# The head of a one-core attention and GeGLU kernel: one 256-column part in place of two quarters, wider dummy matmuls, and three loads moved behind a transpose

## The chip, the cores and the metric

One core of a Trainium2 chip. The metric is device time in microseconds (us), median over executions. Engines are called as in the profile: PE is the matmul engine, PEld its weight loads, DVE and ACT the vector and scalar engines, POOL a third one, SP the engine that issues most DMAs.

## The reference

```python
xn = layernorm(A_x)                                   # x: 2048 x 448
q  = xn @ wq                                          # 16 heads of 256
p  = softmax(q @ k.T / 16)                            # 512 cached keys, 8 kv heads
s  = (p @ v) @ wo
g  = silu((gelu(xn @ w_gate) * (xn @ w_up)) @ w_down) # F = 1792
out = A_x + s * g
```

The part that matters is the start: layernorm of the first tiles of x, their transposition, and the first products with `w_gate` and `w_up`.

## The kernel before

The rows of x are 16 tiles of 128; a chunk is four tiles (512 columns after transposition). A "unit" is one block of 128 columns of `w_gate` and `w_up` for one chunk: 14 matmuls in 7 pairs, where a pair is two 64-row halves that run side by side (at 128 columns they start 18 to 20 ns apart within a group, and each is recorded as 216 ns long). Phase 0 has four pairs, phase 1 three. Units 0 to 3 start before all four tiles of chunk 0 are there: units 0, 1 and 2 are computed tile by tile (quarters of 128 columns), unit 3 in one go at the end.

```python
load_x("sp", 6, 2)
load_w("sp", 3, 0)          # third weights, gate: 480 KB   (wanted by unit 9)
load_w("sp", 3, 1)          # third weights, up:   480 KB
load_x("sp", 8, 4)          # x of chunk 2:        448 KB
# ...
def warm(n, b):             # dummy matmuls that keep PE busy until x has come
    for i in range(n):
        ins = e.matmul(bank[b][:, 0:256], lhsT=gl[:, 0, 0:P], rhs=gl[:, 0, 0:256], ...)
# ...
warm(19, 2)
ln_first(0); ln_first(1); ln_second(0)
ln_tp_pe(0, ((0, 6), (1, 4)))                # transposition on PE, copied out by ACT
warm(2, 2)
# ... quarters (0,1) and (1,2) of units 0, 1, 2, with tiles 1 and 2 transposed between
gu_group(HEAD[:1], PH[:1], (2, 3), (0,))     # unit 0, tile 2, phase 0
ln_a()                                       # statistics of tile 4 (chunk 1)
ln_tp_pe(3, T, "dve")                        # tile 3 transposed on PE, copied out by DVE
ln_a()
ln_b()                                       # tile 4 normalised; DMA transpose issued on SP
gu_group(HEAD[1:], PH[1:], (2, 3), (0,))     # units 1 and 2, tile 2, phase 0
gu_group(HEAD, PH, (2, 3), (1,))             # units 0, 1, 2, tile 2, phase 1
gu_group(HEAD[:2], PH[:2], (3, 4))           # units 0 and 1, tile 3
for ph in range(2):
    gu_group((3,), (6,), None, (ph,))        # unit 3, all 512 columns
    gu_group(HEAD[2:], PH[2:], (3, 4), (ph,))# unit 2, tile 3
# then unit pairs (4,5), (6,7), (8,9), ... in 512 columns
```

The softmax here doesn't subtract the row's maximum and nothing guards it: scores larger than these inputs give would overflow.

Of the kernel before, what the change touches and what calls it, by code (L numbers as in the profile page):

```python
# [11 lines left out]
P = 128  # L12
# [152 lines left out]
def bass_recurrent_scan__sliding_block_cached__geglu_ffn__prompt_kernel(  # L165
# [19 lines left out]
    QC = 512  # L185
# [16 lines left out]
    with es:  # L202
# [3 lines left out]
        def place(name, shape, dt, at=None):  # L206
            size = {BF16: 2, F32: 4}[dt]
            for n in shape[1:]:
                size *= n
            size = (size + 31) // 32 * 32  # L210
            if at is None:
                at = base[0]
                base[0] += size
            assert at + size <= nc.sbuf_usable_end, (name, at + size, nc.sbuf_usable_end)
            return nc.alloc_sbuf_tensor_at(name, list(shape), dt, offset=at), at, at + size
# [69 lines left out]
        gl, a, at = place("gl", [P, NGL, QC], BF16, at=at)  # L285
# [18 lines left out]
        bank = [pall[i // 2][:, (i % 2) * 512:(i % 2) * 512 + 512] for i in range(8)]  # L304
# [9 lines left out]
        def dma(q, o, i, reads=(), writes=()):  # L314
            K.op(q, lambda e, o=o, i=i: e.dma_start(o, i), reads, writes, dma=True)
# [16 lines left out]
        def load_x(q, t0, n):  # L332
            dma(q, x4[:, t0:t0 + n, :], x_view[:, t0:t0 + n, :], (), b_x4[t0:t0 + n])

        def load_w(q, i, j):
            w = (B_w_gate, B_w_up)[j]
            lo, hi = FBL[i] * P, FBL[i + 1] * P
            dma(q, wgu[:, j, :, lo:hi], w[0:K3, lo:hi].rearrange("(k p) f -> p k f", p=P), (), (b_wl[i][j],))
# [27 lines left out]
            load_wr("sp", i, 0)  # L366
            load_wr("sp", i, 1)
        load_x("sp", 6, 2)
        load_w("sp", 3, 0)
        load_w("sp", 3, 1)  # L370
        load_x("sp", 8, 4)


        def ln_bn(t):
# [5 lines left out]
        def ln_stats(t):  # L380
            ln_bn(t)
            ln_aggr(t)

        def ln_rstd_pool(t):
            K.op("pool", lambda e: e.tensor_scalar(
                ve[:, t:t + 1], mv[:, t, 1:2], LN_EPS, None, op0=ALU.add), (b_mv[t],), (b_ve[t],))
            K.op("pool", lambda e: e.tensor_tensor(
                rstd[:, t:t + 1], ve[:, t:t + 1], nhalf[:, :], ALU.pow), (b_ve[t], b_nhalf), (b_rstd[t],))
# [8 lines left out]
        def ln_norm(t, dup="dve"):  # L397
            s = t % NXN

            def nm(lo, hi, src, b):  # L400
                K.op("dve", lambda e: e.tensor_scalar(  # L401
                    xn[:, s, lo:hi], x4[:, t, src:src + hi - lo], mv[:, t, 0:1], rstd[:, t:t + 1],
                    op0=ALU.subtract, op1=ALU.mult), (b_x4[t], b_mv[t], b_rstd[t]), (b,))
            nm(0, D, 0, b_xn[s][0])
            if dup == "dve":
                nm(D, DP, K3, b_xn[s][1])
            else:
                act(xn[:, s, D:DP], xn[:, s, K3:D], ACT.Copy, b_xn[s][:1], b_xn[s][1:])

        def ln_tp_dma(t):  # L410
            s = t % NXN
            dma_t(xnT[:, :, t * P:(t + 1) * P], xn[:, s, :], b_xn[s], b_xnT[t])

        def ln_tp_pe(t, parts, eng="act"):

            s = t % NXN
            for i, b in parts:
                tp = pall[b // 2].bitcast(BF16)[:, :].rearrange("p (b k c) -> p k b c", b=2, c=R)
                ks = {None: slice(0, NK + 1), 0: slice(1, 3), 1: slice(0, 4, 3)}[i]

                def fn(e, tp=tp, ks=ks):
                    ins = None
                    for k in range(NK + 1)[ks]:
                        for u in range(2):
                            r = slice(R * u, R * u + R)
                            ins = e.transpose(tp[:, k, u, :], xn[r, s, k * P:(k + 1) * P], ident[r, r])  # L426
                    return ins
                K.op("pe", fn, (b_xn[s][:1] if i == 0 else b_xn[s]) + [b_ident], b_ps[b:b + 2])
            for i, b in parts:
                tp = pall[b // 2].bitcast(BF16)[:, :].rearrange("p (b k c) -> p k b c", b=2, c=R)  # L430
                ks = {None: slice(0, NK + 1), 0: slice(1, 3), 1: slice(0, 4, 3)}[i]
                o = xnT[:, ks, t * P:(t + 1) * P].rearrange("p k (b c) -> p k b c", c=R)
                bx = b_xnT[t] if i is None else b_xnT[t][i:i + 1]
                if eng == "act":
                    act(o, tp[:, ks, :, :], ACT.Copy, b_ps[b:b + 2], bx)
                else:
                    K.op("dve", lambda e, o=o, i=tp[:, ks, :, :]: e.tensor_copy(o, i), b_ps[b:b + 2], bx)

        last_row = {}

        def warm(n, b):
            def fn(e):
                ins = None
                for i in range(n):
                    ins = e.matmul(bank[b][:, 0:256], lhsT=gl[:, 0, 0:P], rhs=gl[:, 0, 0:256], start=True, stop=True)  # L445
                return ins
            last_row[b] = (K.op("pe", fn, (b_gl[0],), b_ps[b:b + 2]), None)


        def group(units, lo, hi, start, stop, phases=(0, 1)):  # L450





            for p in phases:
                ph, part = p if isinstance(p, tuple) else (p, None)
                ks = {None: [2, 1, 0, NK], 0: [2, 1], 1: [0, NK]}[part]
                for (b, w, wr, cols, reads, rreads, xts) in units:
                    lst = []  # L460
                    for k in ks:
                        if k == NK and ph == 1:
                            continue
                        for u, j in ((0, ph), (1, 1 - ph)):
                            rows = slice(R * u, R * u + R)
                            l = wr[rows] if k == NK else w(j, k)[rows]
                            lst.append((bank[b + j][:, lo:hi], l, xnT[rows, k, cols], start and ph == 0 and k == 2,
                                        stop and ph == 1 and k == 0))
                    before = [last_row[b][0]] if b in last_row and last_row[b][1] != ph else []
                    xb = [y for x in xts for y in (x if part is None else x[part:part + 1])]  # L470
                    rr = rreads if ph == 0 and NK in ks else []
                    o = mms(lst, reads + rr + xb, b_ps[b:b + 2], before)
                    last_row[b] = (o, ph)

        def gu_group(ns, pairs, part=None, phases=(0, 1)):

            lo, hi = (0, QC) if part is None else (part[0] * P, part[1] * P)
            units = []
            for n, b in zip(ns, pairs):
                c, f = divmod(n, NF)  # L480
                wi = [j for j in range(4) if FBL[j] <= f][-1]
                fc = slice(f * P, (f + 1) * P)
                units.append((b, lambda j, k, fc=fc: wgu[:, j, k, fc], wgur[:, fc], slice(c * QC + lo, c * QC + hi),
                              b_wl[wi] + [b_wgu], b_wlr[min(wi, 2)], b_xnT[c * 4 + lo // P:c * 4 + hi // P]))
            group(units, lo, hi, lo == 0, hi == QC, phases)
# [23 lines left out]
        def ln_first(t):  # L509
            ln_stats(t)  # L510
            ln_std_act(t)

        def ln_second(t, dup="dve"):
            ln_recip(t)
            ln_norm(t, dup)
# [3 lines left out]
        def ln_a():  # L519
            if ln_t[0] < NT:  # L520
                ln_stats(ln_t[0])
                ln_rstd_pool(ln_t[0])
                ln_t[0] += 1

        def ln_b():
            if ln_t[1] < ln_t[0]:
                ln_norm(ln_t[1])
                ln_tp_dma(ln_t[1])
                ln_t[1] += 1

        warm(19, 2)
        ln_first(0)
        ln_first(1)
        ln_second(0)
        ln_tp_pe(0, ((0, 6), (1, 4)))
        warm(2, 2)
        ln_second(1, "act")
        HEAD, PH = (0, 1, 2), (0, 2, 4)
        T = ((None, 6),)
# [13 lines left out]

        act(tmp[:, 1, 0:1], nhalf[:, :], ACT.Gelu_apprx_tanh, (b_nhalf,), (b_tmp[1][0],))
        gu_group(HEAD[:1], PH[:1], (2, 3), (0,))
        ln_a()
        ln_tp_pe(3, T, "dve")
        ln_a()
        ln_b()
        gu_group(HEAD[1:], PH[1:], (2, 3), (0,))  # L560
        gu_group(HEAD, PH, (2, 3), (1,))
        gu_group(HEAD[:2], PH[:2], (3, 4))
        for ph in range(2):
            gu_group((3,), (6,), None, (ph,))
            gu_group(HEAD[2:], PH[2:], (3, 4), (ph,))

        def load_k(g):
            dma_t(kT[:, g, :, :], A_k_cache[0, g, Sk - W:Sk, :], (), (b_kT[g],))
# [163 lines left out]
        for i in range(2):  # L732
            b = (AB[3], BB[0])[i]
# [58 lines left out]
```

## Time and profile before

557.23 us, median of 3 (557.22 to 557.56); the profiled execution took 556.87, its span is 555.1.

| | value | read from |
|---|---|---|
| PE busy | 549.7 of 555.1 us | page, part 1 |
| PE's share of the chain that ended last | 98% | page, part 4 |
| last hole in PE on that chain | 0.34 us at 12.59 us | chain in order of time |
| weight loads on either side of the hole | 12.315 and 12.920 us, 0.605 apart | trace |

The page: the span, the busy time of each engine (busy us, share of the span, x instructions), and the shares of the chain of work that ended last.

```profile
span 555.1 us, 9781 instructions
...
PE 549.7 (99%) x3651; PEld 260.1 (47%) x3651; DVE 317.0 (57%) x817; ACT 273.9 (49%) x727; POOL 32.9 (6%) x64
...
PE 98%; DVE 0%; DMA 0%; issue 0%
```

The chain of the kernel before in order of time; columns: start us, length us, what.

```profile
9.75 2.83 PE bank L327 x74
12.59 0.34 issue
12.92 538.82 PE bank L327 x3432
```

After 12.92 us nothing but PE is on the chain until the last 0.6 us. What PE gains before that comes off the end; what it gains later would have to be fewer or shorter matmuls.

The PE timeline of the kernel before at the hole (start us, length us, engine, line, operation, out<-in, form, count, idle before and its releaser), and then the weight loads at the same place.

```profile
12.08 0.39 PE L327 MATMUL bank<-xnT,wgur 64*128 64x512 bf16 x2
12.29 0.29 PE L327 MATMUL bank<-xnT,wgu 64*128 64x128 bf16 x4
12.92 0.23 PE L327 MATMUL bank<-xnT,wgu 64*128 64x128 bf16 x2 [0.34 <-issue]
```

```profile
12.08 0.33 PEld L327 LDWEIGHTS bank<-xnT,wgu 64*128 64x128 bf16 x4
12.92 0.10 PEld L327 LDWEIGHTS bank<-xnT,wgu 64*128 64x128 bf16 x2 [0.51 <-issue]
```

The hole lies between the second and the third pair of one group (unit 2's last quarter, phase 0). In the trace neither the weight loads nor the matmuls of the third pair carry a semaphore wait, so there is nothing to wait for in the program. "issue" says as much: no releaser was found. The pairs start 56 ns apart elsewhere and 0.55 us apart here: the hole costs 0.50 us, more than its 0.34 us of idle time, because a matmul's recorded length (216 ns at 128 columns) runs past the start of the next one (56 ns later).

### The profile page before, as it was taken

The page shows a single profiled execution, that of the slowest core. Times are in us where ns is not written, and L with a number is a line of the kernel's source. Part 1 is how long each engine was busy: PE and PEld are TensorE (multiplying, and loading weights), DVE is VectorE, ACT ScalarE, POOL GpSimd, SP SyncE. Part 2 cuts the span into 40 slices and gives each one's busy share as a digit, 9 for nine tenths or more (in the row PEclk, how much of TensorE's full clock was granted, in tenths as well). Part 3 has the DMA queues.
Part 4 walks back from the last instruction along what each step waited for, and adds up shares of the span by engine and source line. Part 5 has one row for each costly group of instructions (what it writes and reads, how often), then busy time and mean ns, then how long its engine had stood idle before and what let it go on. Part 6 is the DMA issues. An engine that isn't in the chain of part 4 may idle for free.

```text
span 555.1 us, 9781 instructions
## 1 busy us (share of the span) xinstructions
PE 549.7 (99%) x3651; PEld 260.1 (47%) x3651; DVE 317.0 (57%) x817; ACT 273.9 (49%) x727; POOL 32.9 (6%) x64
## 2 busy tenths in 40 slices
PE   8999999999999999999999999999999999999997
PEld 6444444444544444454444445544444454444455
DVE  6773534443485785525858752285785525858722
ACT  5432324353485784505758751085784504758600
POOL 1120830000000000000000000000000000000000
PEclk9999999999999999999999999999999999999999
DMA  9560799703175383313706803176364313707601
GB/s 302 104 164 9 199 277 297 108 1 39 38 134 96 76 149 81 76 35 90 153 20 152 152 21 74 34 145 100 77 151 77 77 34 90 153 20 152 153 8 34
DMA packets 163599, 57.63 MB, mean 104 GB/s; under 512 B 151456, under 2 KB 160672, under 8 KB 163552
## 3 DMA queue, kind: packets, MB, share of 16 engines
q1 hardware_dynamic: 159488, 45.16, 39.9%
q0 software_dynamic: 3296, 11.27, 6.9%
q8 instruction: 29, 0.48, 0.4%
q10 hardware_dynamic: 768, 0.57, 0.3%
q14 instruction: 18, 0.15, 0.1%
HBM read 17.92 MB, written 1.84 MB: 36 GB/s over the span
## 4 chain that ended last, share of the span: by engine, by line
PE 98%; DVE 0%; DMA 0%; issue 0%
PE bank L327 98%; DMA x<-in_A_x_dram 0%; DVE stats L375 0%; PE bank L426 0%; DVE xn L401 0%; DVE mv L378 0%; PE bank L445 0%; DVE tmp L679 0%; DVE ofin L682 0%; DVE rstd L395 0%
## 5 line engine op out<-in xcount | busy, mean ns | idle before, releaser
L640 ACT ACTIVATE p<-bank 128x512 f32<-128x512 f32 x256 | 149.5, 597 | 103.0 <-PE bank L327 99.9
L644 DVE TENSOR_SCALAR pn<-p,rden 128x512 bf16<-128x512 f32 x256 | 124.5, 486 | 16.4 <-DMA pT<-pn 7.6
L327 PE MATMUL bank<-kT,qT 128*128 128x512 bf16 x512 | 121.0, 379 | 0.0
L327 PE MATMUL bank<-pT,va 128*128 128x512 bf16 x512 | 120.8, 379 | 0.0
L327 PE MATMUL bank<-wo,oT 128*128 128x448 bf16 (+2 forms) x544 | 97.7, 341 | 0.0
L327 PE MATMUL bank<-xnT,wq 64*128 64x512 bf16 x768 | 94.7, 376 | 0.0
L327 PE MATMUL bank<-xnT,wgu 64*128 64x512 bf16 (+1 forms) x780 | 83.6, 347 | 0.4 <-issue 0.3
L327 PEld LDWEIGHTS bank<-pT,va 128*128 128x128 bf16 x512 | 50.0, 98 | 60.5 <-DMA pT<-pn 0.7
L327 PEld LDWEIGHTS bank<-kT,qT 128*128 128x128 bf16 x512 | 49.5, 98 | 61.6 <-issue 3.4
L327 PEld LDWEIGHTS bank<-wo,oT 128*128 128x128 bf16 x544 | 52.0, 98 | 45.5
L626 DVE CAST qT<-bank 128x512 bf16<-128x512 f32 x64 | 42.8, 691 | 49.4 <-PE bank L327 49.4
L321 ACT ACTIVATE qT<-bank 128x512 bf16<-128x512 f32 x64 | 38.2, 597 | 61.1 <-PE bank L327 59.5
L327 PEld LDWEIGHTS bank<-xnT,wq 64*128 64x128 bf16 x768 | 36.8, 94 | 46.8 <-ACT p L640 2.1
L321 ACT ACTIVATE gl<-bank 128x512 bf16<-128x512 f32 x56 | 33.1, 597 | 49.8 <-PE bank L327 46.6
L494 DVE TENSOR_TENSOR actT<-bank,gl 128x512 bf16<-128x512 f32 x56 | 37.8, 689 | 34.0 <-PE bank L327 25.3
L327 PEld LDWEIGHTS bank<-xnT,wgu 64*128 64x128 bf16 x780 | 35.3, 94 | 39.0 <-issue 1.3
L643 DVE RECIPROCAL rden<-rsum 128x1 f32<-128x1 f32 x256 | 40.3, 157 | 21.9 <-ACT p L640 21.8
L640 ACT ACTIVATION_READ_ACCUMULATOR p<-bank 128x1 f32 x256 | 52.8, 206 | 0.0
L679 DVE SCALAR_TENSOR_TENSOR tmp<-bank,g 128x448 f32<-128x448 f32 (+2 forms) x17 | 10.1, 596 | 72.2 <-PE bank L327 72.2
L663 DVE CAST oT<-bank 128x512 bf16<-128x512 f32 x64 | 43.7, 683 | 6.9 <-PE bank L327 6.9
L327 PE MATMUL bank<-wd,actT 128*128 128x448 bf16 x224 | 43.0, 353 | 0.0
L321 ACT ACTIVATE oT<-bank 128x512 bf16<-128x512 f32 x64 | 39.2, 612 | 7.0 <-PE bank L327 7.0
(39 smaller groups left out, 183.6 us busy)
## 6 DMA issues: line engine op xcount, KB each, us to landing
wo<-in_A_wo_dram POOLq DMA_DIRECT2D x4, 896.0 KB, 21.0
wq<-in_A_wq_dram POOLq DMA_DIRECT2D x2, 1536.0 KB, 11.4
va<-in_A_v_cache_dram POOLq DMA_DIRECT2D x8, 256.0 KB, 16.6
pT<-pn SPq DMA_TRANSPOSE x128, 2.8
xr<-in_A_x_dram POOLq DMA_DIRECT2D x16, 112.0 KB, 2.3
out_dram<-ofin SPq DMA_DIRECT2D x15, 112.0 KB, 1.7
wd<-in_B_w_down_dram SPq DMA_DIRECT2D x1, 1568.0 KB, 8.3
x<-in_A_x_dram SPq DMA_DIRECT2D x2, 448.0 KB, 5.5
```

The costliest lines, as they stand in the source:

```text
L321: K.op("act", lambda e, o=o, i=i: e.activation(o, i, func, scale=scale), reads, writes)
L327: ins = e.matmul(o, lhsT=l, rhs=r, start=st, stop=sp)
L494: K.op("dve", lambda e: e.tensor_tensor(actT[:, c % 2, f, :], bank[b + 1], gl[:, s, :], ALU.mult), (b_ps[b + 1], b_gl[s]), (b_actT[c % 2][ ...
L626: K.op("dve", lambda v, s=s, b=b: v.tensor_copy(qT[:, s, 1, :], bank[b + 1]), (b_ps[b + 1],), (b_qT[s][1],))
L640: K.op("act", lambda e, b=b, r=r, z=z: e.activation(p32[:, z, :], bank[b], ACT.Exp, scale=att_scale, accum_out=rsum[:, r:r + 1]), (b_ps[b] ...
L643: K.op("dve", lambda e, r=r: e.reciprocal(rden[:, r:r + 1], rsum[:, r:r + 1]), (b_rsum[r],), (b_rden[r],))
L644: K.op("dve", lambda e, r=r, z=z, y=y, t=t4 % 2: e.tensor_scalar(pn[:, y, t, :], p32[:, z, :], rden[:, r:r + 1], None, op0=ALU.mult), (b_p ...
L663: K.op("dve", lambda v, i=i, b=b: v.tensor_copy(oT[:, i, :], bank[b]), (b_ps[b],), (b_oT[i],))
L679: K.op("dve", lambda e: e.scalar_tensor_tensor(out=tmp[:, s, c0:c1], in0=bank[b][:, c0:c1], scalar=0.5, in1=g2[:, t, c0:c1], op0=ALU.mult, ...
```

## The change

Its intent, as the title has it: do unit 2's second half as one 256-column part beside unit 3, use fewer and wider dummies, and keep three large loads out of the DMA queue until chunk 1's first transpose has been issued. The diff, with cuts:

```diff
         load_x("sp", 6, 2)
-        load_w("sp", 3, 0)
-        load_w("sp", 3, 1)
-        load_x("sp", 8, 4)
...
-        def warm(n, b):
+        def warm(n, b, w):
...
-                    ins = e.matmul(bank[b][:, 0:256], ... rhs=gl[:, 0, 0:256], ...)
+                    ins = e.matmul(bank[b][:, 0:w], ... rhs=gl[:, 0, 0:w], ...)
...
-        warm(19, 2)
+        warm(9, 2, QC)
+        warm(1, 2, QC // 2)
...
-        warm(2, 2)
+        warm(2, 2, QC // 2)
...
         gu_group(HEAD[:1], PH[:1], (2, 3), (0,))
-        ln_a()
         ln_tp_pe(3, T, "dve")
         ln_a()
+        ln_a()
         ln_b()
-        gu_group(HEAD[1:], PH[1:], (2, 3), (0,))
-        gu_group(HEAD, PH, (2, 3), (1,))
+        load_w("sp", 3, 0)
+        load_w("sp", 3, 1)
+        load_x("sp", 8, 4)
+        gu_group(HEAD[1:2], PH[1:2], (2, 3), (0,))
+        gu_group(HEAD[:2], PH[:2], (2, 3), (1,))
         gu_group(HEAD[:2], PH[:2], (3, 4))
         for ph in range(2):
             gu_group((3,), (6,), None, (ph,))
-            gu_group(HEAD[2:], PH[2:], (3, 4), (ph,))
+            gu_group(HEAD[2:], PH[2:], (2, 4), (ph,))
```

More of the change, by code (lines that the diff above doesn't have):

```diff
@@ L444, in fn @@
                 for i in range(n):
-                    ins = e.matmul(bank[b][:, 0:256], lhsT=gl[:, 0, 0:P], rhs=gl[:, 0, 0:256], start=True, stop=True)
+                    ins = e.matmul(bank[b][:, 0:w], lhsT=gl[:, 0, 0:P], rhs=gl[:, 0, 0:w], start=True, stop=True)
                 return ins
```

## The prediction

> **What bounds the kernel.** TensorE. The profile page has PE busy 549.7 of 555.1 us (99%), granted clock 0.999. The chain of waits in order of time is PE alone from 12.92 us on (one piece of 538.82 us) and ends with 0.6 us of DVE. Before that stand the first load of x, normalisation of tile 0, and PE work with one hole: 0.34 us of "issue" at 12.59. So only the first 13 us can win, and whatever PE gains there should come off the end nearly whole.
>
> **The hole.** In the PE timeline the fourth and fifth weight loads of unit 2's last quarter, inside one group with no semaphore between them, start 0.605 us apart (12.315, 12.920); the neighbours are 53 ns apart per pair. About 0.5 us is lost. The instruction queue moves 16 KB blocks; its first one ran from 10.46 to 11.60 us, when the data loads kept the DMA engines at 9 tenths. [...] About 450 traced PE instructions precede the hole[...]. The link is my inference.
>
> **The parts, costed.**
> 1. Dummies 19x256 -> 9x512 + 1x256: the same columns. A 256-column dummy takes 213 ns before the clock rises at 4.2 us and 109 after. They end at about 4.7 us; the first transpose starts at 5.38 on xn. No direct time; 18 fewer instructions (matmul and load each) before the hole.
> 2. Unit 2's two 128-column quarters as one 256-column part: a pair of row halves takes 56 ns at 128 columns and, at 215 for 512, about 109 at 256 (estimate). 7 pairs save only about 0.02 us directly, but 28 instructions go, and unit 2's work now stands beside unit 3. By the time instruction ~450 is due, PE will be in unit 4 at about 14.2 us (estimate) instead of 12.4: the block should be there. Gain about 0.5 us.
> 3. Loss: with unit 2 gone from between, columns of tile 3 are wanted at about 10.13 us instead of 10.52. The DVE copy of tile 3, now ahead of a statistics step, starts near 9.80 instead of 9.98, takes 0.39, so PE gets it near 10.3: a new wait of 0.1 to 0.2 us.
> 4. Moved loads: 1.4 MB (two of 480 KB, one of 448) leave the queue at 8.6 to 10.1 us and are issued after chunk 1's first transpose, near 13.9 us. That relieves fetch and transpose. The third weights should land near 18.5 us; PE wants them near 20.3 (unit 9). Off the chain, about 2 us spare.
> 5. Normalisation of tile 4 comes about 0.9 us later (DVE near 12.0 us), so evacuating unit 0 starts near 12.6 instead of 12.08. Unit 4 starts near 13.5 and finds its banks free.
>
> **Sum.** 0.50 + 0.02 - 0.15 = about 0.38 us. 557.23 -> 556.85 us; range 556.5 to 557.3. Faster by over 2%: 0.005; within 2%: 0.99; slower: 0.005.
>
> **What would show it.** The hole is gone; PE reaches the first matmul of unit 4 near 13.5 instead of 13.9 us; a PE wait on the DVE copy of tile 3 near 10.2; PE busy falls by well under 0.1 us; no PE wait near 20 us; the chain is still PE at 98%.
>
> **What would make it wrong.** The hole is not a fetch, or moves rather than vanishes (no gain, or a loss of 0.1 to 0.2). The wait on tile 3 is longer. The third weights land behind the transpose later than 20.3 us and stall unit 9. The clock rises at another phase. The three runs before spread 0.34 us, as much as the effect.

The sum is 0.50 + 0.02 - 0.15 = 0.37, put down as about 0.38 us.

## The result, and the profile after

556.80 us, median of 6 (556.55 to 557.70), against 557.23 us, median of 6, for the kernel before. The ratio is 0.9995 (95% interval 0.9982 to 1.0008). A ratio is the mean time of one kernel's runs over that of the other's in the same rounds, so it is not quite the ratio of the medians. In total, the changed kernel ran 16 times (mean 556.93, 556.53 to 557.81) and the kernel before 38 times (mean 557.14, 556.25 to 557.91). A gain of about 0.2 us in the mean is seen, over several jobs and chips; for the changed kernel no interval of a single job excludes a ratio of 1.

The execution that was profiled happened to be the slowest of the first six, 557.70 us. The same parts of the page for the changed kernel:

```profile
span 555.9 us, 9711 instructions
...
PE 548.2 (99%) x3603; PEld 260.9 (47%) x3628; DVE 317.2 (57%) x817; ACT 274.0 (49%) x727; POOL 32.8 (6%) x64
...
PE 96%; ACT 1%; DMA 1%; issue 1%; DVE 0%; SPq 0%; DVEq 0%
```

The span is 0.8 us longer than before, not shorter. (Of the drop of PE's busy time nothing should be made: 25 matmul records are missing, 3603 where 3628 weight loads are recorded.) The PE timeline of the changed kernel where the hole would be:

```profile
12.25 0.40 PE L327 MATMUL bank<-xnT,wgur 64*128 64x512 bf16 x2
12.47 0.51 PE L327 MATMUL bank<-xnT,wgu 64*128 64x256 bf16 x6
12.80 0.29 PE L327 MATMUL bank<-xnT,wgur 64*128 64x256 bf16 x2
12.90 1.80 PE L327 MATMUL bank<-xnT,wgu 64*128 64x512 bf16 x18
```

No idle time stands in brackets: the hole is gone. But eight microseconds later, in the same timeline:

```profile
20.57 0.40 PE L327 MATMUL bank<-xnT,wgur 64*128 64x512 bf16 x2
21.67 0.82 PE L327 MATMUL bank<-xnT,wgu 64*128 64x512 bf16 x6 [0.71 <-DVE xn L398]
```

This is the first matmul of unit 9, the first user of the third weights. It starts 1.10 us after the pair before it (20.57 to 21.67), where 0.22 is the pace of 512 columns: 0.88 us lost. The view names DVE's `xn`, because a wait for several semaphores is put down to the one that it found last. The matmul waits for the weights, too. The timeline of SP, and the time from issue to landing of the two `wgu` loads (min/median/max), show them:

```profile
12.94 1.31 SPq L318 DMA_TRANSPOSE xnT<-xn  x1
14.30 1.97 SPq L315 DMA_DIRECT2D wgu<-in_B_w_gate_dram  x1
16.32 0.48 SPq L315 DMA_DIRECT2D wgu<-in_B_w_up_dram  x1
16.84 0.49 SPq L315 DMA_DIRECT2D x<-in_A_x_dram  x1
```

```profile
DMA to landing us min/median/max: 5.1/5.2/5.3
```

The load of the up weights starts to be issued at 16.32 and lands 5.26 us later, at 21.58; PE's weight load follows at 21.64. The DVE work that the bracket names had ended at 21.41, 0.2 us earlier. So the releaser was the DMA.

A third thing makes this execution late, and is not one that the change was meant to touch. The statistics step of tile 2 on DVE, first in the kernel before, then in the changed one:

```profile
6.00 0.63 DVE L375 BATCH_NORM_STATS2 stats<-x 128x6 f32<-128x448 bf16 x1
```

```profile
6.26 0.63 DVE L372 BATCH_NORM_STATS2 stats<-x 128x6 f32<-128x448 bf16 x1 [0.28 <-DMA x<-in_A_x_dram]
...
10.13 0.42 DVE L434 COPY xnT<-bank 128x512 bf16<-128x512 bf16 x1 [0.56 <-PE bank L423]
```

The x of tile 2 was issued at 1.65 us in both and landed at 5.98 before and at 6.23 after. This shifts everything behind it: tile 3's transposition starts at 9.46 before and at 9.80 after. (The second line is the copy of tile 3, from 10.13 to 10.55 us; the first matmul that needs it starts at 10.70, after a step of 0.20 us from the last pair where 0.056 is the pace. That is the new wait that was forecast.) To be rid of that shift, I measure from tile 3's transposition (its first PE instruction) to the first matmul of unit 4, which is the stretch that the change rearranges. For the two profiles it is 4.406 and 4.084 us: 0.32 us saved, and then 0.88 us lost at unit 9. The sum of this one execution: -0.32 (the stretch) + 0.34 (the late head) + 0.88 (unit 9) = +0.90, and -0.08 in the 532 us behind unit 10, makes +0.82; the spans differ by 0.82.

### The profile page after: what moved, and what is told of

The parts are those of the page before. It is cut to its first block, busy times and chain, and to the rows that moved or that the text cites. A ratio compares the mean times of both kernels' runs of the same rounds, so it can differ in the third digit from the quotient of the medians.

```text
span 555.9 us, 9711 instructions
## 1 busy us (share of the span) xinstructions
PE 548.2 (99%) x3603; PEld 260.9 (47%) x3628; DVE 317.2 (57%) x817; ACT 274.0 (49%) x727; POOL 32.8 (6%) x64
## 4 chain that ended last, share of the span: by engine, by line
PE 96%; ACT 1%; DMA 1%; issue 1%; DVE 0%; SPq 0%; DVEq 0%
PE bank L327 96%; DMA x<-in_A_x_dram 1%; ACT qT L321 1%; SPq L315 0%; DVE stats L372 0%; ACT gl L321 0%; DVE actT L491 0%; ACT xnT L321 0%; DVE xn L398 0%; DVE tmp L680 0%; ACT ve L388 0%; DVE ofin L683 0%; PE bank L423 0%; DVE mv L375 0%; DVEq L151 0%
## 5 line engine op out<-in xcount | busy, mean ns | idle before, releaser
L327 PE MATMUL bank<-kT,qT 128*128 128x512 bf16 x487 | 117.5, 379 | 2.2 <-ACT qT L321 1.3
L327 PE MATMUL bank<-xnT,wgu 64*128 64x512 bf16 (+2 forms) x768 | 84.0, 350 | 1.0 <-DVE xn L398 0.7
L327 PEld LDWEIGHTS bank<-xnT,wgu 64*128 64x128 bf16 x768 | 36.9, 94 | 38.2 <-DVE xn L398 1.2
## 6 DMA issues: line engine op xcount, KB each, us to landing
va<-in_A_v_cache_dram POOLq DMA_DIRECT2D x8, 256.0 KB, 12.6
```

The lines of the kernel that those rows point to most:

```text
L327: ins = e.matmul(o, lhsT=l, rhs=r, start=st, stop=sp)
```

## The experiments

Twelve runs were made, five timed rounds each; three of them are unedited kernels again. Theory (an inference of mine, put to the test here): the hole is PE waiting for a block of its own instructions that the DMA engines bring late; fewer instructions ahead of that point let PE get there later. Rivals: the hole comes from the place in the program (the step from 512 to 128 columns); or it goes because the moved loads relieve the DMA engines. For unit 9: the wait belongs to the change, or was a chance of one execution.

All 14 profiles, in one table. "Block" is the transfer of the first 16 KB on q8 that falls in the run (the profile lists q8 as "instruction": 29 transfers of 16,384 bytes in the kernel before, as many in the changed one); "hole" is the excess over the pace of the pairs; "recorded PE instr." counts matmuls, weight loads and the few semaphore instructions of PE (438 of the 449 in the first row are matmuls and weight loads); "stretch" is from tile 3's transposition to unit 4; "-" means none seen. The first row and "after" are the two profiles shown above.

```
kernel            block us        hole us, ends at  recorded PE instr. before  stretch  unit 9 waits
before            10.46 - 11.60   0.50,  12.92      449                        4.406    -
before_again       9.86 - 11.03   0.15,  12.56      449                        4.055    -
e_loads_only      11.30 - 12.40   1.42,  13.85      449                        5.327    -
d_short_dummies   10.29 - 11.53   1.78,  13.01      449                        5.649    -
k_short_queue      9.56 - 10.49   -                                            3.996    -
c_dummies_only    10.11 - 11.32   -                                            3.951    -
c_again           10.63 - 11.93   -                                            3.902    -
g_unit2_only      10.18 - 11.28   -                                            4.087    -
after             10.44 - 11.75   -                                            4.084    0.88
a_again           10.55 - 11.77   -                                            4.088    -
a_third           10.46 - 11.66   -                                            4.085    0.20
j_loads_then_tr.  10.84 - 12.03   -                                            4.088    -
b_loads_early     10.68 - 11.86   -                                            4.087    -
q_split_copy      10.40 - 11.62   -                                            4.069    -
```

### The hole: instructions, place or DMA load

**d_short_dummies.** The kernel before with 38 dummies of 128 columns: the same columns, 38 instructions more.

```diff
-        warm(19, 2)
+        warm(38, 2, P)
```

> The kernel before with 38 dummies of 128 columns instead of 19 of 256: the same columns, 38 PE instructions more ahead of everything. Fetch theory: the hole comes 38 instructions (19 matmuls) earlier, in the last columns of unit 1's second phase near 11.2 us, and is longer, 0.8 to 1.7 us, since the block arrives hardly earlier; time 0.3 to 1.2 us over before. Rival (the place): hole unmoved and 0.5 us, time as before.

557.57 us, median of 5 (557.34 to 558.48); ratio 1.0015 (1.0003 to 1.0028), so the whole interval lies above 1. Its PE timeline:

```profile
11.12 0.28 PE L327 MATMUL bank<-xnT,wgu 64*128 64x128 bf16 x4
13.01 1.06 PE L327 MATMUL bank<-xnT,wgu 64*128 64x128 bf16 x12 [1.62 <-issue]
```

The hole moved to 18 matmuls earlier (two semaphore instructions between make up the 38), out of unit 2 to the start of unit 1's second phase, and grew to 1.78 us (slightly more than expected). It stands after 449 recorded PE instructions, the very count of the kernel before, and ends at nearly the same time. The place in the program is ruled out: the count decides where it falls. When it ends goes with the block's transfer, 1.48 us after its end.

**c_dummies_only** and **c_again.** The kernel before with the changed dummies only.

```diff
-        warm(19, 2)
+        warm(9, 2, QC)
+        warm(1, 2, QC // 2)
```

> The kernel before with nothing changed but the 19 dummies of 256 columns, now 9 of 512 and 1 of 256: 18 PE instructions fewer ahead of everything. Fetch theory[...]: the hole leaves unit 2's last quarter, where PE is at its fifth weight load; it would fall 18 instructions later, inside unit 3's second phase, where PE gets at about 13.0 us, so it is shorter than 0.2 us or gone; time 0.3 to 0.5 us under before. Rival (the hole comes from the place, the step from 512 to 128 columns or the bank): still 0.5 us at the fifth weight load of that quarter, time as before.

556.47 us, median (556.26 to 556.63); ratio 0.9992 (0.9979 to 1.0006). No hole; unit 2's last quarter, untouched, runs at pace. 18 instructions fewer were enough here.

> The dummies-only kernel again. Its instruction 449 falls due near 13.1 us, so it escapes only where the block's transfer ends before 11.7 us: a hole of 0 to 0.8 us. Time 556.3 to 557.2 us, 0.2 to 0.5 under before on this chip, more spread than the version with loads early and two copies.

556.83 us, median (556.55 to 557.99); ratio 0.9999 (0.9986 to 1.0011). No hole in the profiled execution, though its block ended late, at 11.93 us: PE is due at instruction 449 near 13.3 us there, 1.4 us after the block, so it escaped by next to nothing. What made 557.99 of another execution was not profiled.

**e_loads_only.** The kernel before with only the three loads moved.

```diff
         load_x("sp", 6, 2)
-        load_w("sp", 3, 0)
-        load_w("sp", 3, 1)
-        load_x("sp", 8, 4)
...
         ln_a()
         ln_b()
+        load_w("sp", 3, 0)
+        load_w("sp", 3, 1)
+        load_x("sp", 8, 4)
         gu_group(HEAD[1:], PH[1:], (2, 3), (0,))
```

> The kernel before with the three loads moved behind the first transpose and nothing else changed. Theory: the block of PE instructions queues behind loads issued before 8 us, so taking away the loads issued at 8.6 us and later does not bring it sooner: its transfer starts near 10.4 us, the hole stays after 449 recorded PE instructions and is 0.3 to 0.6 us. Rival (relieving the DMA engines is what removes the hole): transfer starts before 10 us and the hole is under 0.2 us. In both the third up weights land between 19 and 21 us; PE wants them at 20.9. Time 556.7 to 557.4 us.

556.94 us, median, but 558.44 in the profiled execution (556.63 to 558.44); ratio 0.9996 (0.9984 to 1.0009). Its PE timeline:

```profile
12.30 0.29 PE L327 MATMUL bank<-xnT,wgu 64*128 64x128 bf16 x4
13.85 0.23 PE L327 MATMUL bank<-xnT,wgu 64*128 64x128 bf16 x2 [1.26 <-issue]
```

The hole is in its old place and the longest seen there, 1.42 us, well past the 0.3 to 0.6 expected: the block's transfer started later still, at 11.30 us. Moving the loads neither removed the hole nor brought the block sooner.

**before_again.** The kernel before, unedited.

> The kernel before, unedited, for a second profile of its hole. Theory (the hole lasts until about 1.4 us after the end of the block's transfer, which varies with the DMA engines): the hole is again after 449 recorded PE instructions, of another length than 0.50 us, anywhere from 0 to 1.5 us, ending 1.3 to 1.5 us after the transfer's end; times spread 1 us or more. Rival (fixed): 0.5 us again.

557.11 us, median (556.57 to 557.91); ratio 1.0000 (0.9987 to 1.0013). The hole stands after 449 instructions again and is 0.15 us long. Over the four profiles with a hole it ends 1.32, 1.52, 1.45 and 1.48 us after the transfer's end, while the end itself moves by 1.4 us. That is the fetch theory's mark. That the load on the DMA engines sets this end was not shown: from 9 to 12 us they were busy for a share of 0.86 in e_loads_only, where the block ended last of these four (12.40 us), and of 1.09 here, where it ended first (11.03). The spread of the hole would account for much of the 1.7 us over which the times of the kernel before spread, but only two executions of it were profiled.

**k_short_queue.** The same PE instructions as before, but the second and third weights and x from tile 6 on are issued only when tile 4 has been normalised (11.7 us), ahead of its transpose.

```diff
-        for i in (1, 2):
+        for i in (1,):
...
-        load_x("sp", 6, 2)
-        load_w("sp", 3, 0)
-        load_w("sp", 3, 1)
-        load_x("sp", 8, 4)
...
                 ln_norm(ln_t[1])
+                if ln_t[1] == 4:
+                    load_w("sp", 2, 0, b_xn[4 % NXN])   # waits for the normalised tile
+                    # ... the other loads, in their old order
                 ln_tp_dma(ln_t[1])
```

> The kernel before, same PE instructions, but the loads of the second and third weight blocks and of x from tile 6 on wait for tile 4's normalisation (11.7 us): the DMA queue runs empty near 9 us. Fetch theory: the block of PE instructions starts its transfer 1 us or more sooner, before 9.5 us, and the hole after 449 instructions is gone or under 0.15 us though no PE instruction was moved. Rival (the fetch starts at a set time or instruction, not behind the loads): transfer at 10.1 to 10.7 us, hole 0.4 to 0.6 us. A wait at unit 6 near 17 us or unit 9 near 21 us may eat the gain, so the time decides nothing here.

558.72 us, median (558.09 to 559.63); ratio 1.0024 (1.0011 to 1.0036). The busy time of the engines from 9 to 12 us, first of the kernel before, then of this one (each engine's busy us and count, granted clock, the DMA engines' mean busy share, GB/s):

```profile
9.00:12.00 3.00, 2.94 (x92) 2.47 (x87) 2.61 (x9) 2.21 (x5) 1.50 (x4) 1.00 1.08 360
```

```profile
9.00:12.00 3.00, 2.94 (x100) 2.60 (x96) 2.69 (x9) 2.21 (x4) 1.31 (x4) 1.00 0.02 5
```

With the engines idle the block came earliest of all, at 9.56 to 10.49 us, and there was no hole, with no PE instruction moved. The start missed the 9.5 us that I had set, and it is only 0.30 us ahead of before_again's. So the run agrees with "the block waits behind data" only in part: the last data packet of this run had ended at 8.22 us, 1.34 us before the block began. The kept traces say what else may count. From the third transfer on q8 to the 29th, one comes per 254 recorded PE instructions on average in the kernel before and per 255 in the changed one (single steps 196 to 306 and 180 to 323). And the next three transfers begin, in all 14 profiles, when 445 to 553, 668 to 710 and 924 to 942 recorded PE instructions have started: near 449 and, by an estimate that adds this mean of 255, near 704 and 959. So q8 goes with PE's instructions. By the same estimate, 255 before 449, the first transfer would be called for near instruction 194. I timed 193, which starts within 0.01 us of it in the first profile of each of these two kernels. It started at 8.41 us here and the transfer followed after 1.16 us; in the other 13 profiles it took 1.6 to 3.2 us. This is read from the traces, not tested; why the delay varies between 1.6 and 3.2 us is not settled. The price is seen, too: unit 6 waited 1.8 us for the second weights.

### The 256-column part

**g_unit2_only.** The kernel before with unit 2's part and the order of tile 3's copy as in the change, dummies and loads as before.

```diff
-        ln_a()
         ln_tp_pe(3, T, "dve")
         ln_a()
+        ln_a()
...
-        gu_group(HEAD[1:], PH[1:], (2, 3), (0,))
-        gu_group(HEAD, PH, (2, 3), (1,))
+        gu_group(HEAD[1:2], PH[1:2], (2, 3), (0,))
+        gu_group(HEAD[:2], PH[:2], (2, 3), (1,))
...
-            gu_group(HEAD[2:], PH[2:], (3, 4), (ph,))
+            gu_group(HEAD[2:], PH[2:], (2, 4), (ph,))
```

> The kernel before with the unit 2 part alone (one 256-column part, tile 3 copied first); dummies and loads as before. Fetch theory: instruction 449 falls in unit 2's second phase near 13.4 us, after the block is there, so no hole over 0.15 us; the wait on tile 3's copy costs 0.15 to 0.25 us as in the changed kernel (200 ns between two pairs where 56 is the pace). Time that of the changed kernel with loads early, 556.5 to 556.9 us.

556.72 us, median (556.67 to 557.02); ratio 0.9989 (0.9975 to 1.0002). The hole is gone by this part alone as well. The step before the columns of tile 3 is 199 ns where 56 is the pace. The stretch, free of the hole, is 4.087 us; with the quarters kept it is 3.90 (c_again) to 3.91 (the kernel before with its hole subtracted). So against these the part costs 0.18 us and pays only by what it does to the hole. In c_dummies_only and k_short_queue, also with quarters and without a hole, the stretch was 3.951 and 3.996, because unit 3 began 0.05 and 0.09 us late; against those the part costs 0.09 to 0.14 us.

**q_split_copy.** The changed kernel with its loads early and tile 3's copy in two halves.

```diff
-        ln_tp_pe(3, T, "dve")
+        ln_tp_pe(3, ((0, 6), (1, 6)), "dve")
...
-        gu_group(HEAD[:2], PH[:2], (3, 4))
+        gu_group(HEAD[:2], PH[:2], (3, 4), ((0, 0), (0, 1), 1))
```

> The changed kernel with its loads early again, and the DVE copy of tile 3 in two halves, so that PE starts on the first half. Theory: the 200 ns step before the columns of tile 3 (56 is the pace) falls to 110 or less, no hole, no wait at unit 9; 556.4 to 556.7 us, 0.1 to 0.15 under the version with loads early and one copy, the fastest and narrowest of this job with dummies-only. Rival (that wait costs nothing further on): as with one copy, 556.65.

556.72 us, median (556.47 to 557.09); ratio 0.9994 (0.9981 to 1.0007). The step fell to 141 ns only, and a later one, where PE takes up phase 1, came to 169: the stretch is 4.069, a gain of 0.02 and not 0.1. A miss; it is not clear of the others in time.

### The wait of unit 9

**a_again** and **a_third.** The changed kernel, unedited.

> The changed kernel again, unedited, to see whether the wait of unit 9 in its first profile (0.88 us, ended by the landing of the third up weights at 21.58 us) belongs to it. Theory 1 (the loads stand behind a transpose whose issue and transfer hold them up): the up weights land at 20.5 us or later again and PE waits before unit 9's first matmul, 0.1 us or more. Theory 2 (chance of one execution): they land before 20 us and PE does not wait. Both: no hole of about 0.5 us inside a group near 12 to 14 us. Time 556.6 to 557.0 us, ratio to before 0.9985 to 1.0.

556.86 us, median (556.53 to 556.93); ratio 0.9999 (0.9987 to 1.0012). PE and SP timelines:

```profile
20.64 0.40 PE L327 MATMUL bank<-xnT,wgur 64*128 64x512 bf16 x2
20.86 0.83 PE L327 MATMUL bank<-xnT,wgu 64*128 64x512 bf16 x6
```

```profile
14.34 1.55 SPq L315 DMA_DIRECT2D wgu<-in_B_w_gate_dram  x1
15.94 0.48 SPq L315 DMA_DIRECT2D wgu<-in_B_w_up_dram  x1
```

No wait: the up weights landed at 20.42, between what the two theories had said, 0.4 us ahead of the want at 20.86.

> The changed kernel a third time, on the chip of the other three of this job. No hole near 12 to 14 us. The up weights land between 19.9 and 21.6 us against a want at 20.8: an even chance of a wait at unit 9. Times 556.5 to 557.7, 0.1 to 0.5 over the version with loads early and its tile 3 copy in two.

556.82 us, median (556.75 to 557.81); ratio 1.0000 (0.9987 to 1.0014).

```profile
20.36 0.40 PE L327 MATMUL bank<-xnT,wgur 64*128 64x512 bf16 x2
20.78 0.82 PE L327 MATMUL bank<-xnT,wgu 64*128 64x512 bf16 x6
```

Here the two pairs start 0.42 us apart instead of 0.22: the up weights landed at 20.69, and PE waited 0.20 us. Three profiles, three waits: 0.88, 0 and 0.20 us. It is the change that put the landing on the edge, and chance that decides on which side it falls.

**b_loads_early.** The changed kernel with the three loads put back.

```diff
         load_x("sp", 6, 2)
+        load_w("sp", 3, 0)
+        load_w("sp", 3, 1)
+        load_x("sp", 8, 4)
...
         ln_b()
-        load_w("sp", 3, 0)
-        load_w("sp", 3, 1)
-        load_x("sp", 8, 4)
```

> The changed kernel with the three moved loads put back where they were, everything else kept. Theory 1: third weights land near 16 us, no wait at unit 9; about 0.3 to 0.8 us less time than the changed kernel in any execution where that one waits. If relieving the DMA engines was what removed the hole, the hole comes back (0.3 us or more inside a group, now near unit 4); if the shift of the instruction count removed it, it stays away, and the time is 556.3 to 556.7 us, 0.5 to 0.9 under before.

556.64 us, median (556.49 to 557.02); ratio 0.9997 (0.9984 to 1.0009). The third weights landed at 14.79 and 16.06 us, five ahead of their want; unit 9 does not wait, and there is no hole. The shift of the instruction count alone removes it. The profiled span is 554.8 against 555.9 of the changed kernel's first profile; 0.88 of these 1.15 us are the wait, the rest is the late head.

**j_loads_then_transpose.** The loads wait for the same event as the transpose, but stand ahead of it.

```diff
                 ln_norm(ln_t[1])
+                if ln_t[1] == 4:
+                    load_w("sp", 3, 0, b_xn[4 % NXN])   # waits for the normalised tile
+                    load_w("sp", 3, 1)
+                    load_x("sp", 8, 4)
                 ln_tp_dma(ln_t[1])
...
-        load_w("sp", 3, 0)
-        load_w("sp", 3, 1)
-        load_x("sp", 8, 4)
```

> The changed kernel with the three loads issued at the same moment (they wait for tile 4's normalisation, as the transpose does) but ahead of the first transpose instead of behind it. Theory: the transpose in front costs the loads its issue of 1.3 us and a slow issue of the next load (1.6 to 2.0 us instead of 0.5), so now the up weights land by 18.8 us, unit 9 never waits; time 0 to 0.2 us under the changed kernel, 556.5 to 556.8 us. Rival (the loads are late because they start late, transpose or not): landing 20 us or later.

556.68 us, median (556.55 to 556.84, the narrowest of all); ratio 0.9986 (0.9974 to 0.9999). SP and then PE of this kernel:

```profile
12.70 0.37 SPq L315 DMA_DIRECT2D wgu<-in_B_w_gate_dram  x1
13.12 0.49 SPq L315 DMA_DIRECT2D wgu<-in_B_w_up_dram  x1
13.65 0.49 SPq L315 DMA_DIRECT2D x<-in_A_x_dram  x1
14.18 1.34 SPq L318 DMA_TRANSPOSE xnT<-xn  x1
```

```profile
20.34 0.40 PE L327 MATMUL bank<-xnT,wgur 64*128 64x512 bf16 x2
20.55 0.83 PE L327 MATMUL bank<-xnT,wgu 64*128 64x512 bf16 x6
```

The up weights landed at 19.05 us (I had said 18.8), 1.5 us ahead of the want, against 20.42 to 21.58 behind the transpose. The transpose in front costs its own issue of 1.3 us. In the three profiles of the changed kernel one of the two weight loads also took 1.97, 1.55 and 1.24 us to issue, against 0.37 and 0.49 here. The expectation laid this to the transpose, and that is not borne out: in e_loads_only the loads stand behind the transpose too, and none is slow:

```profile
11.71 1.28 SPq L318 DMA_TRANSPOSE xnT<-xn  x1
13.04 0.57 SPq L315 DMA_DIRECT2D wgu<-in_B_w_gate_dram  x1
13.66 0.48 SPq L315 DMA_DIRECT2D wgu<-in_B_w_up_dram  x1
```

What the three slow issues share is a transfer of the next block of instructions on q8, which began at 14.33, 14.34 and 14.53 us, in the midst of the loads; in e_loads_only it began at 17.04 and here at 16.40. Of 504 plain issues of SP in the 14 profiles, the 472 that did not overlap a transfer of a block on q8 took at most 0.61 us; the five that took longer, 1.24 to 1.97 us, all overlapped one. Which causes which was not tested. The price of this order: the transpose lands at 20.84 instead of 16.6 to 17.3 us, which cost PE nothing that the profile shows.

### A version that may beat both

The means of dummies-only, g, j, b and q were each below that of the kernel before in their jobs (c_again by 0.06 us only). Pooled, the four versions with the 256-column part and without late loads (b, g, j, q; 20 executions on three chips) have a mean of 556.73 and never exceeded 557.09 us; the changed kernel has 556.93 and reached 557.81. This is the direction in which the profiles point, but the versions ran on different chips. Within single jobs only j's interval lies under the kernel before (0.9974 to 0.9999), by about 0.14%; with so many intervals, one that just excludes 1 can be chance. None was taken against the changed kernel itself.

## Why the prediction was right or wrong

The median, 556.80, lies 0.05 us from the forecast 556.85. That closeness is luck: two terms of the sum were off (the hole's size, and a wait at unit 9 that it did not hold), and the noise of a few runs is as large as the effect.

1. *PE bounds, and the first 13 us decide.* Right. From unit 10 on all 14 profiles take 532.1 to 532.8 us to the end.
2. *The hole is a late block of instructions* (marked as an inference). Borne out as far as the runs go: it follows the instruction count (449 in four of four), not the place, and it ends 1.3 to 1.5 us after the block's transfer. Each transfer on q8 is 16,384 bytes, and one comes per 254 to 255 recorded PE instructions (means of two traces). How many instructions PE has at hand, and which block it stood waiting for, was not shown.
3. *0.50 us gained.* Right for the profile at hand, wrong as a size: I took one execution's hole for the kernel's. In three profiles with an unmoved hole (e included, whose loads differ) it is 0.50, 0.15 and 1.42 us.
4. *Dummies: no direct time; unit 2: 0.02 us.* Right for unit 2: pairs of 256 columns start 109 ns apart in the changed kernel, as estimated from 56 at 128 columns and 215 at 512. Instruction 450 came due at 14.3 to 14.6 us, near the forecast 14.2. Not seen in advance: either part alone is enough to clear the hole in the profiles taken. For the dummies "no direct time" is not shown to a tenth: tile 3's transposition starts at 9.53 to 9.86 us in the eight profiles with wider dummies, against 9.43 to 9.46 in the four with the old dummies and the second weights in place. Late x (6.15 us or later: after, a_again, c, c_again) and a late rise of the clock (6.57 us or later: c_again, a_third, q) go with most of it; whether the dummies have a part in it was not tested.
5. *A wait of 0.1 to 0.2 us on tile 3's copy.* Right: the step is 200 ns for 56, and a further 53 ns stand just before it; net of the 0.02 the stretch is 0.18 us longer than without a hole.
6. *Third weights land near 18.5 us against a want of 20.3, "about 2 us spare".* This is the step that failed. They landed at 21.58, 20.42 and 20.69 against wants of 20.79, 20.86 and 20.58 us: a spare of -0.8 to +0.4. The prediction had the issues begin near 13.9 us and the landing 4.6 us later, for both loads together; the first was issued at 14.08 to 14.34, one of the two issues took 1.2 to 2.0 us, and landing took 4.4 to 6.0 us from each load's own issue. The risk was named among those that would make the prediction wrong, and it came true in two of three profiles. With it fell "no PE wait near 20 us", and in the first profile "PE at 98%" of the chain (96%; 98% and 99% in the other two).
7. *That the moved loads relieve fetch and transpose.* Not borne out for the fetch: the block started at 10.44 to 11.30 us with the loads moved (four profiles behind the transpose) and at 9.86 to 10.68 with them in place. The first transpose was relieved (3.9 to 4.4 us from issue to landing in the changed kernel, 4.6 to 6.9 in the eight profiles with the loads in place), but no gain reached PE.
8. *PE at unit 4 near 13.5 us.* 13.88 in the first profile, 13.67 to 13.95 in all three; the head before it was up to 0.4 us later than in the kernel before's first profile, with x of tile 2 landing at 5.92 to 6.30 instead of 5.98 us. The clock's rise goes with it too, as the prediction had feared: it came at 3.84 to 7.10 us over the 14 profiles, with the first dummy always at 1.2 us (in the kernel before the step from one dummy of 256 columns to the next falls from 213 to 109 ns between 4.14 and 4.28 us). In the four profiles in which it rose at 6.57 us or later, tile 1's transposition starts at 6.78 to 7.06 us, in the other ten at 6.49 to 6.70. Tile 4's normalisation and unit 0's evacuation on DVE (forecast 12.0 and 12.6) began at 12.31 and 12.83 us, and no wait at unit 4 came of it.

Open: why the block's transfer starts 1.2 to 3.2 us after instruction 193, near which it seems to be called for by my estimate; why one SP issue takes 1.2 to 2.0 us; how often unit 9 waits; what the slowest executions of versions without a hole did, as no such execution was profiled.

## What to carry to other kernels

A hole in the middle of a group, with "issue" for a releaser, can be the engine waiting for its own instructions, as I infer it was here: count the instructions ahead of it, add a few without work, and see whether the hole follows the count (here it stood after 449 recorded ones in four profiles of three kernels). In this kernel the number of instructions mattered more than their work: with the same columns of dummies the hole was 1.78 us with 38 of 128, 0.50 and 0.15 us with 19 of 256, and not seen in two profiles with 9 of 512 and 1 of 256. So near such a point few wide ones are worth a try, dummies included. Before you move a load behind another DMA, compare landing and want over several executions: a forecast spare of 2 us came out as -0.8 to +0.4 here, and a single profile of an effect this small can show either sign.
